# Attention scores: whole 32-row K tiles against zero-padded query copies, in place of a shifted copy of K

## The chip, the cores and the metric

The kernel runs on one NeuronCore of a Trainium2 chip. The metric is the device time of one execution in microseconds (us). The core has five engines that run in parallel and meet at semaphores: TensorE (PE in the profile) multiplies matrices into the eight banks of PSUM, VectorE (DVE), ScalarE (ACT) and GpSimd (POOL) compute elementwise, and SyncE (SP) here only issues DMAs. In the profile, PEld is the loading of a matmul's stationary operand. The granted clock is the share of its full speed that TensorE was given.

## The reference

Two blocks over the same x (2048 rows, 512 columns, bf16), mixed by a gate per row:

```python
x = A_x
g = _sigmoid((x * gate_w).sum(-1, keepdims=True))
a = _A_ref(x, A_wqkv, A_wo)
b = _B_ref(x, B_wqkv, B_wo)
return g * a + (1 - g) * b
```

A is softmax attention with 32 heads of 16 dimensions:

```python
qkv = (lambda x, *d: x.transpose(*d))((x @ wqkv).reshape(B, S, 3, H, Dh), 2, 0, 3, 1, 4)
q, k, v = qkv[0], qkv[1], qkv[2]
scores = jnp.einsum("bhqd,bhkd->bhqk", q, k) * (Dh ** -0.5)
p = _softmax(scores, axis=-1)
o = jnp.einsum("bhqk,bhkd->bhqd", p, v)
```

B is linear attention with the feature map phi(t) = t + 1 where t > 0, exp(t) elsewhere, plus 1e-6. Both end in an output projection.

## The kernel before

**Layout.** K is kept transposed in KT: four groups (t8) of 128 partitions, eight heads of 16 rows each, for all 2048 keys. A query tile QT holds the same for one group and 512 queries; there are 16 query tiles, counted by q4, in three buffers. A score matmul takes 16 rows of K and of Q, at partitions 0, 32, 64 or 96, so that up to four heads run side by side in the rows of the array, each writing 128 keys x 512 queries into a PSUM bank of its own.

**Two rounds to a query tile.** The four heads that start at partitions 0, 32, 64 and 96 are one round (`par` 0). The other four start at 16, 48, 80 and 112, where a tile of the array cannot begin. For them one DMA per group copies KT, shifted by 16 partitions, into KS (`t_kproj`), and one per query tile copies QT into QS (`t_qproj`); round `par` 1 reads KS and QS (`kq_aps`). A KS copy is made when all four key quarters of a group are projected, so an odd round needs all of them (`kq_keys`). There are 32 rounds of 16 key blocks and four heads: 2048 score matmuls.

**What follows a score.** ACT takes three banks, then two, in turn, and writes exp into a PT buffer (line 806). For some key blocks DVE does the exponential instead: line 982 evicts a bank as scaled integers into Lb, and lines 1004 to 1014 make Eb and Xb from it, so that three products with V (and with a scaled copy VX) together give what PT would. The PV matmuls take 128 keys as rows and 17 columns (16 of V and a one for the sum), four heads side by side in the columns of the array, and accumulate in one bank (`acc`). At the end of a round DVE transposes, divides and gates (`round_end`).

**The order** is not written by hand. While the program is built, a planner holds a clock for each engine with fixed costs, and picks what TensorE does next: score groups for ACT first, then scores for DVE, PV, products for DVE's blocks, and projections and all of block B as tasks with a due time and an earliest time, both counted in rounds. A query tile is due at 2 q4 - 0.9. Where the next pick lies in the future and fewer than WARMC columns were streamed in the last 3.413 us of the planner's clock, it emits a dummy: four PV-shaped matmuls on a tile of zeros (`emit_dummy`, tile sb_warm), which add zero. The plan is fixed in the program; on the chip each engine runs its own list in order and waits at semaphores.

Of the kernel before, what the change touches and what calls it, by code (L numbers as in the profile page):

```python
# [145 lines left out]
def bass_gated_mix__mha_block__linear_attn_block__prompt_kernel(  # L146
# [26 lines left out]
    with ExitStack() as es:  # L173
# [33 lines left out]
        identb = SB("identb", [128, 128], BF16)  # L207
        pidx_i = SB("pidx_i", [128, 1], I32)
        pidx = SB("pidx", [128, 1], FP32)
        mtmp = SB("mtmp", [128, 8], FP32)  # L210
# [40 lines left out]
        r_KT = [[R(f"KT{a}_{t}") for t in range(4)] for a in range(4)]  # L251
        r_KS = [R(f"KS{a}") for a in range(4)]
        r_QT = [R(f"QT{a}") for a in range(3)]
        r_QS = [R(f"QS{a}") for a in range(3)]
        r_V = [[R(f"V{k}_{g}") for g in range(2)] for k in range(NTB)]
# [124 lines left out]
        op(PO, lambda: nc.gpsimd.memset(warm, 0.0), writes=[r_warm])  # L380
        op(PO, lambda: nc.gpsimd.memset(dummy[:], 0.0), writes=[r_dummy])  # L381
        op(PO, lambda: nc.gpsimd.memset(identb[:], 0.0), writes=[r_ident])
# [4 lines left out]
        op(PO, lambda: nc.gpsimd.iota(pidx_i[:], [[0, 1]], base=0, channel_multiplier=1), writes=[r_mask])  # L387
        op(PO, lambda: nc.gpsimd.tensor_copy(pidx[:], pidx_i[:]), reads=[r_mask], writes=[r_mask])
        for j in range(8):
# [39 lines left out]
        def t_kproj(t8, t):  # L429
            if t8 == 0:  # L430
                lhs, wr = (lambda cc: wA0[:, 0, cc, :]), r_wA0
            else:
                lhs, wr = (lambda cc: wA[:, 1, cc, 128 * t8:128 * (t8 + 1)]), r_wA[1]
            b = yield "bank"
            yield from proj_steps(b, lhs, lambda cc: xT[:, cc, 512 * t:512 * (t + 1)], [r_xT[c][t] for c in range(NCC)] + [wr])
            yield ("dve", [r_bk[b]], [])
            op(DV, lambda: nc.vector.tensor_copy(KT[:, t8, 512 * t:512 * (t + 1)], BK[b]), reads=[r_bk[b]],  # L437
               writes=[r_KT[t8][t]], cost=0.69)
            yield "free"
            if t == 3:  # L440
                dma(KS[0:112, t8, :], KT[16:128, t8, :], f"ks{t8}", reads=r_KT[t8], writes=[r_KS[t8]], lat=4)

        def t_qproj(qc, t8):
            s = (4 * qc + t8) % 3
            if t8 == 0 and qc == 0:
                lhs, wr = (lambda cc: wA0[:, 1, cc, :]), r_wA0
# [3 lines left out]
            yield from proj_steps(b, lhs, lambda cc: xT[:, cc, 512 * qc:512 * (qc + 1)], [r_xT[c][qc] for c in range(NCC)] + [wr])  # L450
            yield ("dve", [r_bk[b]], [r_QT[s]])
            op(DV, lambda: nc.vector.tensor_copy(QT[:, s, :], BK[b]), reads=[r_bk[b]], writes=[r_QT[s]], cost=0.69)
# [185 lines left out]
        DLAT, DGRACE = 10.5, 2.0  # L638
        WARMC = 3400.0

# [410 lines left out]
        for t in range(NQC):  # L1051
            add(("xtr", t), t_xtr(t), 0.25 * t - 0.3)
            add(("K", 0, t), t_kproj(0, t), 0.25 * t - 0.2, pre=[("xtr", t)] + ([("K", 0, k) for k in range(3)] if t == 3 else []))
            if t == 0:
# [8 lines left out]
        for t8 in range(1, 4):  # L1063
            for t in range(4):
                add(("K", t8, t), t_kproj(t8, t), 2 * t8 - 0.9 + 0.1 * t, 2 * t8 - 1.8 + 0.2 * t,
                    pre=XT + ([("K", t8, k) for k in range(3)] if t == 3 else []))
        for q4 in range(1, 16):
# [150 lines left out]
```

## Time and profile before

| | |
|---|---|
| Times of the runs | 1076.32 and 1089.12 us, median 1082.72 |
| Profiled execution | 1079.47 us, span in its trace 1077.7 us |
| Busy share of the span | PE 92%, ACT 77%, DVE 63%, weight loads 19%, POOL 2% |
| Mean granted clock of TensorE | 0.587 of full |
| Score matmuls | 1024 on QT and KT, 1024 on QS and KS, mean 553 and 568 ns |
| Exponentials on ACT | 687 instructions, 815.9 us |
| Blocks of exponentials on DVE | 83, with 332 score tiles |
| Dummy matmuls | 516 |
| DMA | 16.39 MB, 16 engines mostly idle |

Busy times overlap, since the engines run side by side. Matmuls are pipelined: four tiles side by side each show some 0.4 to 0.6 us, and the busy time of a group counts a stretch once. A share over the whole span is a mean over stretches that may be limited by different things. Some records of matmuls can be missing from a trace; the weight loads show how many there were.

### The profile page before, as it was taken

The numbers are of one execution on the slowest core, as the hardware profiler recorded it, in microseconds if no ns is written. First come the engines' busy times: TensorE is split into PE (matmuls) and PEld (weight loads), VectorE is DVE, ScalarE is ACT, GpSimd is POOL, SyncE is SP. The second block draws the span as 40 slices with busy tenths as digits, with TensorE's granted clock in tenths as the row PEclk, the third lists the DMA queues.
The fourth block names the chain that finished last, engine by engine and source line by source line (L and its number), as shares of the span: only waits on it lengthen the run. The fifth ranks groups of instructions, "written<-read, shape, count | busy, mean of one in ns | idle before, by whom it ended". The sixth has DMA issues, their size and how long they took to land. (4 is left out here: it accounts for less than half of the span.)

```text
span 1077.7 us, 14346 instructions
## 1 busy us (share of the span) xinstructions
PE 993.1 (92%) x6101; PEld 209.9 (19%) x6164; DVE 678.0 (63%) x1003; ACT 833.3 (77%) x722; POOL 17.5 (2%) x43
## 2 busy tenths in 40 slices
PE   6999899899998998998989999999999999899998
PEld 2312111111111111212112112222221211111112
DVE  2335766676767667745556667766665664766775
ACT  4874787887877878968777888958877787687995
POOL 2101100000000000000000000000000000000000
PEclk9755855655555556658655555865585655655556
DMA  7000000000000000001001000000000000000000
GB/s 190 18 5 17 5 18 1 22 1 5 1 5 1 1 5 2 25 1 44 1 1 44 1 6 9 21 16 1 17 18 15 3 16 17 10 5 18 4 1 20
DMA packets 29487, 16.39 MB, mean 15 GB/s; under 512 B 16944, under 2 KB 28976, under 8 KB 29424
## 3 DMA queue, kind: packets, MB, share of 16 engines
q1 hardware_dynamic: 25232, 13.64, 4.6%
q10 hardware_dynamic: 4192, 1.84, 0.7%
q8 instruction: 48, 0.79, 0.3%
q14 instruction: 15, 0.12, 0.0%
HBM read 6.55 MB, written 2.10 MB: 8 GB/s over the span
## 5 line engine op out<-in xcount | busy, mean ns | idle before, releaser
L806 ACT ACTIVATE sb_PT<-ps 128x1536 bf16<-128x1536 f32 (+1 forms) x687 | 815.9, 1248 | 212.1 <-PE ps L357 207.0
L982 DVE TENSOR_SCALAR sb_Lb<-ps 128x512 uint16<-128x512 f32 x332 | 225.0, 689 | 270.8 <-PE ps L357 269.5
L357 PE MATMUL ps<-sb_QT,sb_KT 16*128 16x512 bf16 x1024 | 240.9, 553 | 17.7 <-ACT sb_PT L806 11.8
L357 PE MATMUL ps<-sb_QS,sb_KS 16*128 16x512 bf16 x1024 | 240.2, 568 | 14.4 <-ACT sb_PT L806 11.8
L357 PE MATMUL ps<-sb_PT,sb_V 128*17 128x512 bf16 x1716 | 236.8, 554 | 8.9 <-DVE sb_U L879 8.3
L1014 DVE TENSOR_TENSOR sb_Xb<-sb_Xb,sb_Lb 128x2048 bf16<-128x2048 bf16 x83 | 101.6, 1224 | 2.4
L1011 DVE TENSOR_TENSOR sb_Xb<-sb_Xb 128x2048 bf16<-128x2048 bf16 x83 | 101.1, 1219 | 0.0
L357 PEld LDWEIGHTS ps<-sb_QT,sb_KT 16*128 16x128 bf16 x1024 | 42.6, 98 | 213.0 <-ACT sb_PT L806 100.2
L357 PEld LDWEIGHTS ps<-sb_PT,sb_V 128*17 128x17 bf16 x1716 | 41.3, 91 | 198.8 <-issue 174.2
L357 PEld LDWEIGHTS ps<-sb_QS,sb_KS 16*128 16x128 bf16 x1024 | 41.4, 98 | 197.2 <-ACT sb_PT L806 96.9
L357 PE MATMUL ps<-sb_warm 128*17 128x512 bf16 (+1 forms) x524 | 74.2, 602 | 1.3 <-POOL sb_dummy L381 1.3
L1007 DVE TENSOR_SCALAR sb_Eb<-sb_Lb 128x2048 uint16<-128x2048 uint16 x83 | 57.0, 686 | 0.0
L1004 DVE TENSOR_SCALAR sb_Xb<-sb_Lb 128x2048 uint16<-128x2048 uint16 x83 | 56.7, 683 | 0.0
L357 PE MATMUL ps<-sb_Lb,sb_V 128*17 128x512 bf16 x332 | 48.1, 576 | 6.0 <-DVE sb_Lb L982 5.4
L357 PE MATMUL ps<-sb_Xb,sb_VX 128*17 128x512 bf16 x332 | 48.1, 570 | 4.1 <-DVE sb_Xb L1014 4.1
L357 PE MATMUL ps<-sb_Eb,sb_V 128*17 128x512 bf16 x332 | 49.0, 580 | 1.0 <-DVE sb_Eb L1007 0.9
L357 PE MATMUL ps<-sb_xT,sb_wA 128*128 128x512 bf16 x92 | 41.2, 556 | 5.4 <-issue 3.4
L357 PE MATMUL ps<-sb_wBx,sb_xT 128*128 128x512 bf16 x50 | 25.9, 608 | 4.7 <-issue 2.3
L879 DVE STREAM_TRANSPOSE sb_U<-ps 128x512 f32<-128x512 f32 x32 | 22.8, 711 | 10.4 <-PE ps L357 10.1
L357 PE MATMUL ps<-sb_wA,sb_xT 128*128 128x128 bf16 (+1 forms) x128 | 27.7, 362 | 1.7 <-DVE sb_Lb L982 1.7
L357 PE MATMUL ps<-sb_phiK,sb_xnat 128*128 128x512 bf16 x56 | 26.6, 581 | 2.6 <-issue 2.0
L437 DVE CAST sb_KT<-ps 128x512 bf16<-128x512 f32 x16 | 11.0, 689 | 27.4 <-PE ps L357 27.4
(74 smaller groups left out, 377.2 us busy)
## 6 DMA issues: line engine op xcount, KB each, us to landing
out_dram<-sb_wA SPq DMA_DIRECT2D x16, 128.0 KB, 1.7
sb_QS<-sb_QT SPq DMA_DIRECT2D x16, 112.0 KB, 2.1
sb_KS<-sb_KT SPq DMA_DIRECT2D x4, 448.0 KB, 3.4
sb_xnat<-in_A_x_dram ACTq DMA_DIRECT2D x2, 512.0 KB, 5.2
sb_wA<-in_A_wqkv_dram SPq DMA_DIRECT2D x2, 512.0 KB, 5.3
sb_wBx<-in_B_wqkv_dram SPq DMA_DIRECT2D x2, 512.0 KB, 5.3
sb_xnat<-in_A_x_dram SPq DMA_DIRECT2D x2, 512.0 KB, 3.9
sb_phiK<-sb_wA SPq DMA_TRANSPOSE x64, 2.2
```

Of the source, the lines that this page charges most:

```text
L357: return lambda: nc.tensor.matmul(o, lhsT=l, rhs=r, start=start, stop=stop, skip_group_check=sg)
L437: op(DV, lambda: nc.vector.tensor_copy(KT[:, t8, 512 * t:512 * (t + 1)], BK[b]), reads=[r_bk[b]], writes=[r_KT[t8][t]], cost=0.69)
L806: op(AC, lambda: nc.scalar.activation(PT[:, slot, 0:512 * n], ps[:, 512 * set_[0]:512 * (set_[0] + n)], ACT.Exp, scale=SCALE), reads=wr, w ...
L879: op(DV, lambda: nc.vector.transpose(U[:], acc), reads=[r_acc], writes=[r_U], cost=0.69)
L982: ev = op(DV, lambda: nc.vector.tensor_scalar(Lb[:, sl, 512 * j:512 * (j + 1)], BK[b], S1A, S1B, op0=ALU.mult, op1=ALU.add), reads=[r_bk[b ...
L1004: ev = op(DV, lambda: nc.vector.tensor_scalar(X, L, 0x7F, 0x3F80, op0=ALU.bitwise_and, op1=ALU.bitwise_or), reads=[rl], writes=[rx], cost= ...
L1007: ev = op(DV, lambda: nc.vector.tensor_scalar(E_, L, 0xFF80, None, op0=ALU.bitwise_and), reads=[rl], writes=[re_], cost=CH[1])
L1011: ev = op(DV, lambda: nc.vector.tensor_tensor(xb, xb, xb, ALU.mult), reads=[rx], writes=[rx], cost=CH[2])
L1014: ev = op(DV, lambda: nc.vector.tensor_tensor(xb, xb, lb, ALU.mult), reads=[rx, rl], writes=[rx], cost=CH[3])
```

## The change

**Scores.** KS and QS go. A score matmul now takes all 32 rows of a K tile, which are two heads, for both rounds (`kq_aps`). The query side is QP, with two copies per query tile: in copy p only the 16 rows of the heads of round p hold the query, the other 16 of each 32 are zero, so the other head's rows add nothing.

**How QP is filled.** QP is set to zero once at the start. For 15 of the 16 query tiles, DVE copies the projection into a staging buffer QT (now two), and eight DMAs from SP's queue lay strips of 16 rows into the two copies. The very first tile is written without DMA, by two DVE multiplications with 0/1 masks of the rows, which four small DVE instructions make from an index that POOL now produces earlier.

**Dependencies and planner.** An odd round needs only the quarter of K that it reads, and the last quarter of a group no longer waits for the other three. WARMC goes from 3400 to 3550. The planner then makes another plan.

```diff
@@ SBUF tiles, start @@
-        KS = SB("KS", [128, 4, S], BF16)
-        QT = SB("QT", [128, 3, 512], BF16)
-        QS = SB("QS", [128, 3, 512], BF16)
+        QT = SB("QT", [128, 2, 512], BF16)
+        QP = SB("QP", [128, 3, 2, 512], BF16)
+        maskp = SB("maskp", [128, 2], FP32)
...
+        op(DV, lambda: nc.vector.memset(QP[:], 0.0), writes=[x for v in r_QP for x in v], cost=0.9)
+        op(DV, lambda: nc.vector.tensor_scalar(pidx_j[:], pidx_i[:], 16, None, op0=ALU.bitwise_and),
+           reads=[r_mask], writes=[r_maskp])
+        op(DV, lambda: nc.vector.tensor_copy(maskp[:, 0:1], pidx_j[:]), reads=[r_maskp], writes=[r_maskp])
...
@@ t_kproj @@
-            if t == 3:
-                dma(KS[0:112, t8, :], KT[16:128, t8, :], f"ks{t8}", reads=r_KT[t8], writes=[r_KS[t8]], lat=4)
@@ t_qproj @@
-            yield ("dve", [r_bk[b]], [r_QT[s]])
-            op(DV, lambda: nc.vector.tensor_copy(QT[:, s, :], BK[b]), reads=[r_bk[b]], writes=[r_QT[s]], cost=0.69)
+            if n == 0:
+                yield ("dve", [r_bk[b], r_maskp], [])
+                for p in range(2):
+                    op(DV, lambda p=p: nc.vector.tensor_scalar(QP[:, s, p, :], BK[b], maskp[:, p:p + 1], None, op0=ALU.mult),
+                       reads=[r_bk[b], r_maskp], writes=[r_QP[s][p]], cost=0.69)
+                yield "free"
+                return
+            yield ("dve", [r_bk[b]], [r_QT[st]])
+            op(DV, lambda: nc.vector.tensor_copy(QT[:, st, :], BK[b]), reads=[r_bk[b]], writes=[r_QT[st]], cost=0.69)
             yield "free"
-            dma(QS[0:112, s, :], QT[16:128, s, :], f"qs{s}", reads=[r_QT[s]], writes=[r_QS[s]], lat=2.5)
+            for p in range(2):
+                for j in range(4):
+                    lo = 32 * j + 16 * p
+                    dma(QP[lo:lo + 16, s, p, :], QT[lo:lo + 16, st, :], f"qp{s}_{p}", reads=[r_QT[st]],
+                        writes=[r_QP[s][p]] if j == 0 else [], lat=2.5)
+                r_QP[s][p].w = _Raw(dma_sems[f"qp{s}_{p}"][0], dma_sems[f"qp{s}_{p}"][1], SP.clock + 2.5)
+                r_QP[s][p].r = {}
@@ planner @@
-        WARMC = 3400.0
+        WARMC = 3550.0
...
-            return [("K", t8, kb // 4) if par == 0 else ("K", t8, 3), ("Q", qc, t8)]
+            return [("K", t8, kb // 4), ("Q", qc, t8)]
...
-            if par == 0:
-                return (KT[32 * j:32 * j + 16, t8, 128 * kb:128 * (kb + 1)], QT[32 * j:32 * j + 16, s, :], [r_KT[t8][kb // 4], r_QT[s]])
-            return (KS[32 * j:32 * j + 16, t8, 128 * kb:128 * (kb + 1)], QS[32 * j:32 * j + 16, s, :], [r_KS[t8], r_QS[s]])
+            return (KT[32 * j:32 * j + 32, t8, 128 * kb:128 * (kb + 1)], QP[32 * j:32 * j + 32, s, par, :],
+                    [r_KT[t8][kb // 4], r_QP[s][par]])
```

**How the lists of the engines move.** First TensorE, in the fourth round, at one of block B's first projections (sb_wBx); sb_PT, sb_Lb and sb_Eb are the PV products, sb_warm the dummies. Before:

```order
L357 MATMUL ps<-sb_wBx,sb_xT 128x512 x4
L357 MATMUL ps<-sb_QS,sb_KS 128x512 x4
L357 MATMUL ps<-sb_PT,sb_V 17x512 x4
L357 MATMUL ps<-sb_QS,sb_KS 128x512 x6
L357 MATMUL ps<-sb_PT,sb_V 17x512 x4
L357 MATMUL ps<-sb_Lb,sb_V 17x512 x4
L357 MATMUL ps<-sb_QS,sb_KS 128x512 x2
L357 MATMUL ps<-sb_PT,sb_V 17x512 x4
L357 MATMUL ps<-sb_Eb,sb_V 17x512 x4
L357 MATMUL ps<-sb_warm 17x512 x8
```

After, TensorE at the same place:

```order
L358 MATMUL ps<-sb_wBx,sb_xT 128x512 x4
L358 MATMUL ps<-sb_QP,sb_KT 128x512 x4
L358 MATMUL ps<-sb_PT,sb_V 17x512 x4
L358 MATMUL ps<-sb_QP,sb_KT 128x512 x3
L358 MATMUL ps<-sb_warm 17x512 x4
L358 MATMUL ps<-sb_QP,sb_KT 128x512 x3
L358 MATMUL ps<-sb_PT,sb_V 17x512 x4
L358 MATMUL ps<-sb_Lb,sb_V 17x512 x4
L358 MATMUL ps<-sb_QP,sb_KT 128x512 x2
L358 MATMUL ps<-sb_PT,sb_V 17x512 x4
L358 MATMUL ps<-sb_Eb,sb_V 17x512 x4
L358 MATMUL ps<-sb_warm 17x512 x4
```

The work is the same; one dummy has moved ahead into the six scores. Over the program the dummies go from 516 to 588 matmuls, and the scores for DVE's blocks from 332 to 328.

Second SP, whose whole list is DMAs, after the loads of the inputs. Before:

```order
L302 DMA sb_QS<-sb_QT 112x512
L302 DMA sb_KS<-sb_KT 112x2048
L302 DMA sb_QS<-sb_QT 112x512
L302 DMA sb_KS<-sb_KT 112x2048
L302 DMA sb_QS<-sb_QT 112x512
L302 DMA sb_KS<-sb_KT 112x2048
L302 DMA sb_QS<-sb_QT 112x512
L302 DMA sb_KS<-sb_KT 112x2048
L302 DMA sb_QS<-sb_QT 112x512 x4
L302 DMA sb_wBx<-in_B_wqkv_dram 128x4x512
```

After, SP from the same place, up to the loads of the output weights:

```order
L303 DMA sb_QP<-sb_QT 16x512 x56
L303 DMA sb_wBx<-in_B_wqkv_dram 128x4x512
L303 DMA sb_xnat<-in_A_x_dram 128x8x256 x2
L303 DMA sb_QP<-sb_QT 16x512 x16
L303 DMA sb_phiK<-in_A_wo_dram 128x4x512
L303 DMA sb_phiK<-in_B_wo_dram 128x4x512
```

Eight query copies and four K copies ahead of the reload of sb_wBx become 56 strips for seven query tiles; the first tile needs none.

Third DVE, from its first instruction on; sb_QP is the query copies, sb_maskp and sb_pidx_j the masks. Before:

```order
L397 MEMSET ps 128x512
L398 MEMSET sb_V 128x512
L425 COPY sb_xT<-ps 128x512 x2
L437 CAST sb_KT<-ps 128x512
L452 CAST sb_QT<-ps 128x512
L465 CAST sb_V<-ps 128x4x8x16
```

After, DVE at the same place:

```order
L398 MEMSET ps 128x512
L399 MEMSET sb_QP 128x1536
L400 TENSOR_SCALAR sb_pidx_j<-sb_pidx_i 128x1
L402 CAST sb_maskp<-sb_pidx_j 128x1
L403 TENSOR_SCALAR sb_maskp<-sb_maskp 128x1
L405 TENSOR_SCALAR sb_maskp<-sb_maskp 128x1
L407 MEMSET sb_V 128x512
L434 COPY sb_xT<-ps 128x512 x2
L446 CAST sb_KT<-ps 128x512
L462 TENSOR_SCALAR sb_QP<-ps,sb_maskp 128x512 x2
L486 CAST sb_V<-ps 128x4x8x16
```

Five instructions come in ahead of the first copy of x, and the first query takes two instructions where it took one.

More of the change, by code (lines that the diff above doesn't have):

```diff
@@ L208, in bass_gated_mix__mha_block__linear_attn_block__prompt_kernel @@
         pidx_i = SB("pidx_i", [128, 1], I32)
+        pidx_j = SB("pidx_j", [128, 1], I32)
         pidx = SB("pidx", [128, 1], FP32)
@@ L251, in bass_gated_mix__mha_block__linear_attn_block__prompt_kernel @@
         r_KT = [[R(f"KT{a}_{t}") for t in range(4)] for a in range(4)]
-        r_KS = [R(f"KS{a}") for a in range(4)]
-        r_QT = [R(f"QT{a}") for a in range(3)]
-        r_QS = [R(f"QS{a}") for a in range(3)]
+        r_QT = [R(f"QT{a}") for a in range(2)]
+        r_QP = [[R(f"QP{a}_{p}") for p in range(2)] for a in range(3)]
+        r_maskp = R("maskp")
         r_V = [[R(f"V{k}_{g}") for g in range(2)] for k in range(NTB)]
@@ L381, in bass_gated_mix__mha_block__linear_attn_block__prompt_kernel @@
         op(PO, lambda: nc.gpsimd.memset(dummy[:], 0.0), writes=[r_dummy])
+        op(PO, lambda: nc.gpsimd.iota(pidx_i[:], [[0, 1]], base=0, channel_multiplier=1), writes=[r_mask])
         op(PO, lambda: nc.gpsimd.memset(identb[:], 0.0), writes=[r_ident])
@@ L386, in bass_gated_mix__mha_block__linear_attn_block__prompt_kernel @@
         op(PO, lambda: nc.gpsimd.memset(ones[:], 1.0), writes=[r_const])
-        op(PO, lambda: nc.gpsimd.iota(pidx_i[:], [[0, 1]], base=0, channel_multiplier=1), writes=[r_mask])
         op(PO, lambda: nc.gpsimd.tensor_copy(pidx[:], pidx_i[:]), reads=[r_mask], writes=[r_mask])
@@ L439, in t_kproj @@
             yield "free"
-            if t == 3:
-                dma(KS[0:112, t8, :], KT[16:128, t8, :], f"ks{t8}", reads=r_KT[t8], writes=[r_KS[t8]], lat=4)
         def t_qproj(qc, t8):
-            s = (4 * qc + t8) % 3
-            if t8 == 0 and qc == 0:
+            n = 4 * qc + t8
+            s, st = n % 3, n % 2
+            if n == 0:
                 lhs, wr = (lambda cc: wA0[:, 1, cc, :]), r_wA0
@@ L1052, in bass_gated_mix__mha_block__linear_attn_block__prompt_kernel @@
             add(("xtr", t), t_xtr(t), 0.25 * t - 0.3)
-            add(("K", 0, t), t_kproj(0, t), 0.25 * t - 0.2, pre=[("xtr", t)] + ([("K", 0, k) for k in range(3)] if t == 3 else []))
+            add(("K", 0, t), t_kproj(0, t), 0.25 * t - 0.2, pre=[("xtr", t)])
             if t == 0:
@@ L1065, in bass_gated_mix__mha_block__linear_attn_block__prompt_kernel @@
                 add(("K", t8, t), t_kproj(t8, t), 2 * t8 - 0.9 + 0.1 * t, 2 * t8 - 1.8 + 0.2 * t,
-                    pre=XT + ([("K", t8, k) for k in range(3)] if t == 3 else []))
+                    pre=XT)
         for q4 in range(1, 16):
```

5 lines of the change are left out of this document (added).

## The prediction

> **What bounds the kernel now.** First the page: the share of each engine, the slices and the chain of waits.
>
> ```profile
> span 1077.7 us, 14346 instructions
> PE 993.1 (92%) x6101; PEld 209.9 (19%) x6164; DVE 678.0 (63%) x1003; ACT 833.3 (77%) x722; POOL 17.5 (2%) x43
> PEclk9755855655555556658655555865585655655556
> PE 36%; ACT 6%; DVE 3%; issue 1%
> ```
>
> TensorE is busy for 92% and leads the chain, yet at what clock: most slices stand at five tenths. So I read the busy time of each engine in stretches cut where the granted clock changes; the columns are the stretch, its length, PE, weight loads, DVE, ACT, POOL, the granted clock, DMA share and GB/s. The first sum is over ten stretches at full clock, of which the first, the last and one between are shown; the second is over six at half clock, with the last of them.
>
> ```profile
> 14.00:38.00 24.00, 20.58 (x213) 9.33 (x214) 7.69 (x15) 22.14 (x20) 1.59 (x3) 1.00 0.34 107
> 683.20:707.00 23.80, 21.94 (x169) 5.77 (x168) 16.53 (x23) 23.49 (x23) 0.00 (x0) 1.00 0.09 24
> 925.50:935.70 10.20, 8.67 (x77) 2.50 (x77) 8.59 (x15) 7.75 (x8) 0.00 (x0) 1.00 0.05 14
> sum 136.10, PE 116.81 PEld 35.97 DVE 93.11 ACT 126.77 POOL 1.59; mean PE 11.68 PEld 3.60 DVE 9.31 ACT 12.68 POOL 0.16
> ...
> 935.80:1068.00 132.20, 125.78 (x805) 23.09 (x805) 93.18 (x133) 111.44 (x95) 0.00 (x0) 0.50 0.03 6
> sum 587.80, PE 553.01 PEld 102.70 DVE 396.56 ACT 472.81 POOL 0.00; mean PE 92.17 PEld 17.12 DVE 66.09 ACT 78.80 POOL 0.00
> ```
>
> At half clock PE is full and ACT, which does the exponentials, works 472.81 / 587.80 = 80% of the time; at full clock PE has room and ACT works 93%, in the second row 99%. The kernel has two regimes: PE-bound at half clock, for most of the run, and ACT-bound at full clock. What decides is the clock, so I looked for what raises it. The clock changes only at edges 3.41 us apart; three such windows at half clock, each with the row behind it that shows what it earned:
>
> ```profile
> 335.00:338.41 3.41, 3.39 (x30) 0.72 (x30) 2.14 (x5) 2.20 (x2) 0.00 (x0) 0.50 0.00 0
> 338.41:341.82 3.41, 2.04 (x23) 0.54 (x23) 3.03 (x4) 2.72 (x4) 0.00 (x0) 1.00 0.02 5
> 591.00:594.41 3.41, 3.41 (x30) 0.65 (x23) 1.64 (x4) 2.52 (x3) 0.00 (x0) 0.50 0.00 0
> 594.41:597.83 3.42, 3.01 (x25) 0.61 (x21) 3.42 (x5) 3.23 (x3) 0.00 (x0) 0.50 0.01 2
> 922.09:925.51 3.42, 3.04 (x22) 0.70 (x23) 2.35 (x2) 0.00 (x0) 0.00 (x0) 0.50 0.02 5
> 925.51:928.92 3.41, 3.41 (x34) 1.06 (x33) 2.86 (x6) 0.97 (x2) 0.00 (x0) 1.00 0.00 0
> ```
>
> The first and second both hold 30 matmuls and a full PE; one is followed by the full clock, the other is not. The third has fewer matmuls and an idle gap, and the clock rises. What they consist of, by groups, window by window (a group counts a matmul that reaches over an edge):
>
> ```profile
> L357 PE MATMUL ps<-sb_PT,sb_V 128*17 128x512 bf16 x16 | 2.1, 614 | 0.8 <-DVE sb_U L879 0.8
> L357 PE MATMUL ps<-sb_QS,sb_KS 16*128 16x512 bf16 x10 | 1.4, 550 | 0.0
> L357 PE MATMUL ps<-sb_Lb,sb_V 128*17 128x512 bf16 x4 | 0.6, 632 | 0.0
> ...
> L357 PE MATMUL ps<-sb_QS,sb_KS 16*128 16x512 bf16 x14 | 2.1, 614 | 0.0
> L357 PE MATMUL ps<-sb_PT,sb_V 128*17 128x512 bf16 x12 | 1.5, 620 | 0.0
> L357 PE MATMUL ps<-sb_Lb,sb_V 128*17 128x512 bf16 x4 | 0.6, 632 | 0.0
> ...
> L357 PE MATMUL ps<-sb_warm 128*17 128x512 bf16 x12 | 1.5, 632 | 0.0
> L357 PE MATMUL ps<-sb_phiK 128*128 128x512 bf16 x1 | 0.6, 634 | 0.3 <-issue 0.3
> L357 PE MATMUL ps<-sb_Eb,sb_V 128*17 128x512 bf16 x4 | 0.6, 597 | 0.8 <-DVE sb_Eb L1007 0.8
> L357 PE MATMUL ps<-sb_Xb,sb_VX 128*17 128x512 bf16 x4 | 0.4, 388 | 0.0
> ```
>
> Call 512 columns over the whole array a wave: four PV tiles (17 columns, 128 rows each) are one, a whole-array matmul is one, and four score tiles (16 rows each) count w. The first window has 5 + 2.5 w and rises; the second 4 + 3.5 w and does not; the third has 5 waves of tiles, three of them the dummies, plus one or two whole matmuls, and rises. With w = 1 the second would have 7.5 and stay cold where the third rises on little over 6. So w is below 1, and w = 0.5 fits all three (6.25, 5.75, 6.1 or more) with a threshold of about 6 waves per window. Half is what 16 rows of a 32-row tile are. The dummies are all zeros and still count, so it is active rows, not values.
>
> **The change part by part.** *Score tiles.* Each reads 32 rows instead of 16, the extra ones zero in the query. Their own duration should not move:
>
> ```profile
> L357 PE MATMUL ps<-sb_QT,sb_KT 16*128 16x512 bf16 x1024 | 240.9, 553 | 17.7 <-ACT sb_PT L806 11.8
> L357 PE MATMUL ps<-sb_QS,sb_KS 16*128 16x512 bf16 x1024 | 240.2, 568 | 14.4 <-ACT sb_PT L806 11.8
> L357 PE MATMUL ps<-sb_PT,sb_V 128*17 128x512 bf16 x1716 | 236.8, 554 | 8.9 <-DVE sb_U L879 8.3
> L357 PE MATMUL ps<-sb_warm 128*17 128x512 bf16 x516 | 70.6, 602 | 0.0
> L357 PE MATMUL ps<-sb_Eb,sb_V 128*17 128x512 bf16 x332 | 49.0, 580 | 1.0 <-DVE sb_Eb L1007 0.9
> ```
>
> 16-row tiles take 553 to 568 ns and 128-row tiles 554: rows cost no time. What moves is w, to 1 if active rows are what counts. Tiles: 2048 + 1716 + 516 + 3 x 332 = 5276, or 1319 waves; the 825 other recorded matmuls I take as 500 waves (many are short). Before, with w = 0.5: 1819 - 256 = 1563 waves in 1077.7 / 3.41 = 316 windows, 4.95 each, well under 6. After: 18 dummy waves more (588 dummy matmuls in the program against 516), some 1835, which at the old pace are 5.8 per window, at the edge, so that cold windows now and then pass (the second window above would have 7.5), and at a pace of 925 us 6.8, above it. The half clock can no longer hold for long and the full clock can, though attention-only stretches stay near 6 and will fall back at times. I take the cold state to be left in one window of three and the warm one lost in one of nine: a warm share of 0.75. The bounds are 0.5 and 1.
>
> *The sum.* ACT's work is 833.3 us, and one block of DVE exponentials goes back to it (328 tiles in the program instead of 332): four tiles at 1462 / 3 = 487 ns, 1.9 us, so 835.2, of which 1.6 lie in the first row below.
>
> ```profile
> L806 ACT ACTIVATE sb_PT<-ps 128x1536 bf16<-128x1536 f32 x343 | 501.6, 1462 | 144.8 <-PE ps L357 142.8
> 0.00:16.00 16.00, 8.64 (x34) 3.31 (x35) 3.20 (x6) 1.62 (x3) 5.54 (x29) 1.00 0.99 230
> 1066.00:1077.70 11.70, 8.38 (x39) 3.35 (x36) 4.96 (x9) 0.00 (x0) 0.00 (x0) 0.88 0.13 45
> 112.80 1.02 ACT L806 ACTIVATE sb_PT<-ps 128x1024 bf16<-128x1024 f32 x1 [14.41 <-PE ps L357]
> ```
>
> Outside it lie 16.0 us of start, 11.7 of end and one gap of 14.4 while PE does a row of V projections, which I put at 10 at the faster clock. What is left of before, 1077.7 - 42.1 = 1035.6, holds 136.1 at a share of 0.93 and so 899.5 at (833.3 - 1.6 - 126.8) / 899.5 = 0.784. After, with a warm share of 0.945 (between the mean of 0.93 and the 0.99 of the longest), 0.75 x 0.945 + 0.25 x 0.784 = 0.905, and 833.6 / 0.905 = 921. With 37.7 of start, end and gap: 959. The profiled execution took 1079.47 us, 1.8 above its span, and lies 0.3% under the median of 1082.72: forecast 961. Bounds, with the same 39.5 around them: warm throughout at 0.985, 846 and so 886; half the time at 0.93, 833.6 / 0.857 = 973 and so 1012.
>
> *Query strips.* Eight DMAs from SP in place of one, for 15 of the 16 query tiles; the four K copies go.
>
> ```profile
> 501.85 0.69 DVE L452 CAST sb_QT<-ps 128x512 bf16<-128x512 f32 x1 [1.54 <-PE ps L357]
> 502.57 0.52 SPq L302 DMA_DIRECT2D sb_QS<-sb_QT  x1
> sb_QS<-sb_QT SPq DMA_DIRECT2D x16, 112.0 KB, 2.1
> 538.14 0.10 PEld L357 LDWEIGHTS ps<-sb_QT,sb_KT 16*128 16x128 bf16 x1
> 5.84 0.42 DVE L425 COPY sb_xT<-ps 128x512 bf16<-128x512 bf16 x1 [2.21 <-PE ps L422]
> ```
>
> Issue costs 8 x 0.52 = 4.2 us and the last lands 2.1 later: 6.3 us after the cast at 501.85. The tile cast there is first loaded at 538.14, some 35 us on; at the faster clock that shrinks to 30 and still covers it. Behind the strips on SP stand the next strips, three reloads of weights and inputs, output transposes and stores, none of which a row shows PE waiting for. Cost 0; without cover, 15 x 6.3 = 95 us. Odd rounds no longer ask for all of K; no row shows PE waiting for that copy, so it gains 0. *Start.* The memset of QP and four mask operations fit before the copy at 5.84, ahead of which DVE idled 2.21 us; the first query costs a second 0.69 us on DVE, behind the half that round 0 needs. Between 0 and 2 us, taken as 0.
>
> **The rivals.** *The clock does not move.* Row tiling itself could be what counts half, however many rows; no 32-row tile is in the trace to exclude it. Then PE stays the bound and the 18 dummy waves cost up to 70.6 / 129 = 0.55 us each, 10 us: 1089. Chance 0.11. The Trainium skill speaks for this case (TensorE: Matmul & The Clock Gate, Part 1): it has the clock released by how busy PE has been in windows of about 3.4 us, and asks only for PE without long gaps. By that rule rows would change nothing and the sum would be the 1089 of this case, by the row reading 961. The trace bears out the window and contradicts the rest: PE was busy 125.78 of 132.20 us at 0.50.
>
> *Rows count, but the full clock does not hold* in the attention stretches: warm share 0.25 to 0.5, 1012 to 1060. Chance 0.06.
>
> *Slower: tiles stop overlapping.* In the score waves of TensorE, four 16-row tiles run side by side; 32-row tiles fill their row groups to the border, and a weight load for one could hold up its neighbour. With 512 waves, 42 ns each are 21.6 us, the 2% from which it decides; 0.2 us each are 103 us, 1180. Against it: PV tiles fill all 128 rows of their columns, and 30 tiles of either kind, some 0.6 us each, fit into one window of 3.41 us. Chance 0.04.
>
> **How the numbers follow.** The forecast, rows counted and the clock mostly full, has 0.79, its own range 886 to 1012. 2% is about what a measurement of this kernel tells from no change, so faster means under 1061: 0.79 + 0.06 = 0.85; same 0.11; slower 0.04. The range from 895 to 1060 leaves out 0.11 + 0.04 and some 0.04 of the forecast's fast end.
>
> **What would show it.** The mean granted clock near 0.85 instead of a little under 0.6; the score groups' mean well under 500 ns instead of 560; ACT at 85 to 88% of the span; half-clock stretches of a few windows, mostly between rounds without projections; no idle time put down to the QP DMAs. A clock near 0.6 with w still 0.5 refutes the reading of rows; a full clock with ACT under 90% in it refutes the sum.

## The result, and the profile after

The changed kernel takes 928.59 us (median of two runs, 926.35 and 930.83) against 1082.72: a ratio of 0.8576, with a 95% interval of 0.8341 to 0.8812. It lies inside the forecast's own range and 32 us under the 961. The profiled execution is the run of 930.83, 1.8 us above its span; its mean granted clock is 0.838 where it was 0.587. Ratios, here and below, compare the faster executions of each kernel alone, while the times are medians over all of them, so a ratio can differ a little from the quotient of the two times.

First the page of the changed kernel: busy time of each engine, the clock in 40 slices, the chain of waits, and four groups.

```profile
span 929.0 us, 14661 instructions
PE 801.4 (86%) x6228; PEld 203.3 (22%) x6228; DVE 670.8 (72%) x1001; ACT 809.3 (87%) x723; POOL 16.6 (2%) x43
PEclk9989889979687867789757999997788789977856
ACT 56%; PE 34%; DVE 7%; issue 2%; DMA 1%; ACTq 0%; DVEq 0%
L826 ACT ACTIVATE sb_PT<-ps 128x1536 bf16<-128x1536 f32 (+1 forms) x688 | 796.9, 1306 | 93.9 <-PE ps L358 91.9
L358 PE MATMUL ps<-sb_QP,sb_KT 32*128 32x512 bf16 x2048 | 357.6, 444 | 84.5 <-ACT sb_PT L826 73.6
L358 PE MATMUL ps<-sb_PT,sb_V 128*17 128x512 bf16 x1720 | 192.6, 449 | 10.1 <-DVE sb_U L899 8.5
L358 PE MATMUL ps<-sb_warm 128*17 128x512 bf16 (+1 forms) x596 | 63.9, 466 | 1.3 <-POOL sb_dummy L382 1.3
```

PE does the same work and more dummies in 801.4 us instead of 993.1, and every kind of matmul shares in it: PV tiles, which the change does not touch, go from 554 to 449 ns. That is a clock, not a cheaper instruction. The chain of waits now runs mostly through ACT (56%, before 6%), and most of PE's idle time is waiting for ACT to hand back a bank (73.6 of 84.5 us ahead of the scores, before 23.6 of 32.1).

Next the same kernel cut where the granted clock changes: the sum over all stretches at full clock, the sum over all at half, both from 16.0 us on; then the rows of start and end. The columns are those of the stretches shown before. The trace's record of the clock begins at 16.0 us (at 14.2 us in the kernel before), and what lies ahead of it is printed as 1.00: that figure in the row of the start is no reading (weight loads come every 0.43 us there, the pace of half clock, as the last section shows), and it lifts the mean clocks by up to 0.01.

```profile
sum 612.62, PE 503.44 PEld 143.82 DVE 469.86 ACT 569.51 POOL 8.53; mean PE 14.81 PEld 4.23 DVE 13.82 ACT 16.75 POOL 0.25
...
sum 300.42, PE 289.84 PEld 56.34 DVE 196.72 ACT 238.31 POOL 2.55; mean PE 8.78 PEld 1.71 DVE 5.96 ACT 7.22 POOL 0.08
...
0.00:16.00 16.00, 8.09 (x25) 3.07 (x26) 4.19 (x10) 1.49 (x2) 5.51 (x29) 1.00 1.00 194
917.00:929.00 12.00, 9.09 (x36) 3.52 (x36) 4.95 (x9) 0.00 (x0) 0.00 (x0) 0.85 0.13 45
```

And the gap of ACT while the V projections run, in its timeline (start, length, in brackets the idle time ahead):

```profile
94.09 2.54 ACT L826 ACTIVATE sb_PT<-ps 128x1024 bf16<-128x1024 f32 x2 [11.69 <-PE ps L358]
```

And of the kernel before, all stretches at full clock and all at half, where the prediction had only ten and six of them (from 14.2 us on):

```profile
sum 172.64, PE 140.94 PEld 43.55 DVE 120.83 ACT 146.67 POOL 7.16; mean PE 7.83 PEld 2.42 DVE 6.71 ACT 8.15 POOL 0.40
...
sum 890.88, PE 844.78 PEld 163.46 DVE 554.69 ACT 685.12 POOL 4.77; mean PE 49.69 PEld 9.62 DVE 32.63 ACT 40.30 POOL 0.28
```

The full clock went from 172.64 of 1063.5 us to 612.62 of 913.0 us. Inside each state PE is much as it was: at half clock 844.78 / 890.88 = 95% busy before and 289.84 / 300.42 = 96% after, at full clock 82% in both. What the change moved is how long each state lasts.

### The profile page after: what moved, and what is told of

It is laid out like the page before. It is cut to its first block, busy times and chain, and to the rows that moved or that the text cites. A ratio compares the mean times of both kernels' runs of the same rounds, so it can differ in the third digit from the quotient of the medians.

```text
span 929.0 us, 14661 instructions
## 1 busy us (share of the span) xinstructions
PE 801.4 (86%) x6228; PEld 203.3 (22%) x6228; DVE 670.8 (72%) x1001; ACT 809.3 (87%) x723; POOL 16.6 (2%) x43
## 4 chain that ended last, share of the span: by engine, by line
ACT 56%; PE 34%; DVE 7%; issue 2%; DMA 1%; ACTq 0%; DVEq 0%
ACT sb_PT L826 54%; PE ps L358 34%; DVE sb_Lb L1002 2%; ACT sb_ebuf L528 1%; DMA sb_OT<-in_A_wqkv_dram 1%; DVE sb_Xb L1034 1%; DVE sb_Xb L1031 1%; DVE sb_U L899 1%; DVE sb_Eb L1027 0%; DVE sb_wA L646 0%; DVE sb_xnat L532 0%; DVE sb_Xb L1024 0%; DVE sb_ebuf L530 0%; DVE sb_V L495 0%; DVE sb_phiK L532 0%
## 5 line engine op out<-in xcount | busy, mean ns | idle before, releaser
L826 ACT ACTIVATE sb_PT<-ps 128x1536 bf16<-128x1536 f32 (+1 forms) x688 | 796.9, 1306 | 93.9 <-PE ps L358 91.9
L358 PE MATMUL ps<-sb_QP,sb_KT 32*128 32x512 bf16 x2048 | 357.6, 444 | 84.5 <-ACT sb_PT L826 73.6
L358 PE MATMUL ps<-sb_PT,sb_V 128*17 128x512 bf16 x1720 | 192.6, 449 | 10.1 <-DVE sb_U L899 8.5
L358 PEld LDWEIGHTS ps<-sb_QP,sb_KT 32*128 32x128 bf16 x2048 | 79.1, 93 | 381.8 <-ACT sb_PT L826 263.1
L358 PE MATMUL ps<-sb_warm 128*17 128x512 bf16 (+1 forms) x596 | 63.9, 466 | 1.3 <-POOL sb_dummy L382 1.3
L358 PE MATMUL ps<-sb_Xb,sb_VX 128*17 128x512 bf16 x328 | 38.0, 453 | 11.1 <-DVE sb_Xb L1034 10.9
L358 PE MATMUL ps<-sb_Eb,sb_V 128*17 128x512 bf16 x328 | 38.0, 453 | 2.4 <-DVE sb_Eb L1027 2.2
L528 ACT ACTIVATE sb_ebuf<-ps 128x512 f32<-128x512 f32 x32 | 21.4, 669 | 3.0 <-PE ps L358 3.0
L646 DVE CAST sb_wA<-ps 128x512 bf16<-128x512 f32 x16 | 10.9, 688 | 16.1 <-PE ps L358 16.1
L358 PE MATMUL ps<-sb_phiK 128*128 128x512 bf16 x64 | 21.5, 439 | 0.0
```

What stands on the lines that cost most here:

```text
L358: return lambda: nc.tensor.matmul(o, lhsT=l, rhs=r, start=start, stop=stop, skip_group_check=sg)
L528: op(AC, lambda: nc.scalar.activation(ebuf[:, s, :], BK[b], ACT.Exp), reads=[r_bk[b]], writes=[r_e[s]], cost=0.68)
L646: op(DV, lambda: nc.vector.tensor_copy(outt[:, sl, :], BK[b]), reads=[r_bk[b]], writes=[r_outt[sl], r_wA[2]], cost=0.69)
L826: op(AC, lambda: nc.scalar.activation(PT[:, slot, 0:512 * n], ps[:, 512 * set_[0]:512 * (set_[0] + n)], ACT.Exp, scale=SCALE), reads=wr, w ...
```

## The experiments

The theory: a matmul counts for the clock by the rows of the array that it fills, so that a 16-row score counts half of what it streams and a 32-row one all of it; a window of 3.41 us with about 6 counted waves earns the full clock for the next. Rivals: the new plan and its other DMAs and dummies bring the gain; or PE's busy time decides, whatever it streams; or what counts is the values that pass, not the rows.

### The change without its rows

The changed kernel with its lists, strips and dummies as they are, but score matmuls that read 16 rows. In odd rounds the upper heads' scores are thereby replaced by those of the lower ones.

```diff
-            return (KT[32 * j:32 * j + 32, t8, 128 * kb:128 * (kb + 1)], QP[32 * j:32 * j + 32, s, par, :],
-                    [r_KT[t8][kb // 4], r_QP[s][par]])
+            return (KT[32 * j:32 * j + 16, t8, 128 * kb:128 * (kb + 1)], QP[32 * j:32 * j + 16, s, 0, :],
+                    [r_KT[t8][kb // 4], r_QP[s][0], r_QP[s][par]])
```

> The changed kernel with its instruction lists unchanged on every engine, except that every score matmul reads 16 rows in place of 32, of the even heads in both rounds (odd heads' scores are replaced by the even heads', so the attention of odd heads is not computed). Theory A, active rows set the clock: back to the half clock, mean granted clock 0.57 to 0.63, a score tile weighs 0.5, and the time returns to 1070 to 1100 us. Rival B, the gain comes from the new plan, its 18 more dummy waves, the freed order of K and the strips: all of them are still there, so 920 to 940 us and a clock of 0.83.

Measured: 1079.52 us against 1069.25 for the kernel before on the same chip, a ratio of 1.0017 (0.9823 to 1.0211). Its page:

```profile
span 1056.1 us, 14591 instructions
PE 969.4 (92%) x6167; PEld 208.6 (20%) x6228; DVE 675.2 (64%) x1001; ACT 831.8 (79%) x723; POOL 16.6 (2%) x43
PEclk9798558555585555556655555766568565855556
PE 71%; ACT 18%; DVE 7%; issue 2%; DMA 1%; ACTq 0%; DVEq 0%
L358 PE MATMUL ps<-sb_QP,sb_KT 16*128 16x512 bf16 x2048 | 428.9, 547 | 32.9 <-ACT sb_PT L826 25.7
```

The lists are instruction for instruction those of the changed kernel, and the whole gain is gone: the clock is back at 0.619, the chain back on PE. Plan, strips, masks and the 72 dummies more are together worth nothing that this comparison can see. Two windows at half clock show it in small, each with the row behind it, and then the groups of matmuls in the first. The changed kernel, windows:

```profile
94.53:97.94 3.41, 3.41 (x30) 0.67 (x26) 2.09 (x5) 2.88 (x3) 0.00 (x0) 0.50 0.00 0
97.94:101.36 3.42, 3.42 (x28) 1.00 (x25) 1.78 (x3) 3.39 (x4) 0.00 (x0) 1.00 0.00 0
```

Its groups:

```profile
L358 PE MATMUL ps<-sb_PT,sb_V 128*17 128x512 bf16 x16 | 2.2, 605 | 0.0
L358 PE MATMUL ps<-sb_QP,sb_KT 32*128 32x512 bf16 x10 | 1.8, 592 | 0.0
L358 PE MATMUL ps<-sb_Lb,sb_V 128*17 128x512 bf16 x4 | 0.6, 632 | 0.0
```

The 16-row kernel, windows:

```profile
870.27:873.68 3.41, 3.41 (x30) 0.69 (x26) 2.64 (x5) 2.98 (x3) 0.00 (x0) 0.50 0.00 0
873.68:877.09 3.41, 3.37 (x24) 0.64 (x23) 3.38 (x4) 3.13 (x4) 0.00 (x0) 0.50 0.02 5
```

Its groups:

```profile
L358 PE MATMUL ps<-sb_PT,sb_V 128*17 128x512 bf16 x16 | 2.0, 552 | 0.0
L358 PE MATMUL ps<-sb_QP,sb_KT 16*128 16x512 bf16 x10 | 1.8, 603 | 0.0
L358 PE MATMUL ps<-sb_Lb,sb_V 128*17 128x512 bf16 x4 | 0.6, 632 | 0.0
```

Both windows hold 16 + 10 + 4 matmuls and a PE busy for all of 3.41 us; the one with 32 rows earns the full clock, the one with 16 does not. One such pair is an illustration, no proof: a group counts matmuls that reach over an edge, and the prediction's first window had these same counts with 16 rows and did rise. Cut at the edges, it held 20 PV tiles and 7.3 scores, this one 16 and 9.3: 5.9 and 5.2 counted waves. Hence the count over all windows, further down.

### The rows without the rest of the change

The kernel before, its plan and its shifted copies as they are, but score matmuls of 32 live rows. Each score is then the sum over two heads. Two memsets on POOL at the start fill the rows that the copies leave unwritten with zeros, so that in odd rounds one tile in four has 16 live rows.

```diff
+        op(PO, lambda: nc.gpsimd.memset(QS[96:128], 0.0), reads=[r_const], writes=r_QS)
+        op(PO, lambda: nc.gpsimd.memset(KS[96:128], 0.0), reads=[r_QS[0]], writes=r_KS)
...
-                return (KT[32 * j:32 * j + 16, t8, 128 * kb:128 * (kb + 1)], QT[32 * j:32 * j + 16, s, :], [r_KT[t8][kb // 4], r_QT[s]])
-            return (KS[32 * j:32 * j + 16, t8, 128 * kb:128 * (kb + 1)], QS[32 * j:32 * j + 16, s, :], [r_KS[t8], r_QS[s]])
+                return (KT[32 * j:32 * j + 32, t8, 128 * kb:128 * (kb + 1)], QT[32 * j:32 * j + 32, s, :], [r_KT[t8][kb // 4], r_QT[s]])
+            return (KS[32 * j:32 * j + 32, t8, 128 * kb:128 * (kb + 1)], QS[32 * j:32 * j + 32, s, :], [r_KS[t8], r_QS[s]])
```

> The kernel before with its lists unchanged on PE, DVE, ACT and SP, except that score matmuls read 32 rows of KT, QT, KS and QS without zeros (each score becomes the sum over two heads, so the attention's values change; two memsets on GpSimd at the start fill the last 16 rows of the shifted copies). Theory A: the clock rises as in the changed kernel, mean 0.78 to 0.84, and the time falls to 930 to 970 us, a little above the changed kernel because 18 dummy waves are missing. If in addition only zero-padded rows did something, or the plan did (rival B): 1075 to 1095 us at a clock of 0.59.

Measured: 911.40 us, a ratio of 0.8645 (0.8532 to 0.8759); clock 0.872, from its page:

```profile
span 905.2 us, 14350 instructions
PE 758.6 (84%) x6101; PEld 203.1 (22%) x6164; DVE 673.6 (74%) x1003; ACT 804.0 (89%) x722; POOL 25.0 (3%) x45
PEclk8879879999985899889978888799899899957968
```

The rows alone give the whole gain, with the old copies and 516 dummies. The time lies below the 930 to 970 us that were expected: that 72 dummies are missing cost nothing that shows here. With the run above it is settled from both sides: the rows are needed and they suffice.

### Three quarters of the rows, and rows without zeros

Two runs ask what it is about the rows. The first takes 24 of them (in odd rounds half of each head's dimensions are left out). The second makes the strips carry all 32 rows of the projection, so that no row of the query is zero and each score is the sum over two heads; for that the masks of the first tile become one as well (not shown below). Beside it the changed kernel itself ran again on the second one's chip.

```diff
-            return (KT[32 * j:32 * j + 32, t8, 128 * kb:128 * (kb + 1)], QP[32 * j:32 * j + 32, s, par, :],
+            return (KT[32 * j:32 * j + 24, t8, 128 * kb:128 * (kb + 1)], QP[32 * j:32 * j + 24, s, par, :],
```

> The changed kernel with its lists unchanged, score matmuls over 24 of the 32 rows (in even rounds the result is the same, in odd rounds half of each head's dimensions are left out). Theory A with every active row counting (a score tile weighs 0.75): between the two, 980 to 1030 us, clock 0.68 to 0.76. If a tile counts as a whole from some number of rows on: 925 to 940 us when 24 is enough, 1070 to 1100 us when only all 32 do.

```diff
-                    dma(QP[lo:lo + 16, s, p, :], QT[lo:lo + 16, st, :], f"qp{s}_{p}", reads=[r_QT[st]],
+                    dma(QP[32 * j:32 * j + 32, s, p, :], QT[32 * j:32 * j + 32, st, :], f"qp{s}_{p}", reads=[r_QT[st]],
```

> The changed kernel with its lists unchanged, but the strips carry all 32 rows and the first tile's masks are one, so that no row of a query copy is zero (each score is the sum over two heads). If only active rows count, whatever they hold: the time of the changed kernel within 1%, 905 to 930 us, clock 0.82 to 0.86. If zeros count for less, which would explain why the kernel before with 32 live rows ran at 0.872: 895 to 912 us, clock 0.86 to 0.89.

> The changed kernel itself, as the measure for the runs beside it. 905 to 930 us, clock 0.82 to 0.86, a warm share of about two thirds.

Measured: 24 rows 1026.82 us, ratio 0.9661 (0.9412 to 0.9911), clock 0.666, between 16 rows (0.619) and 32 (0.838), though in the traced execution below the 0.68 that was expected at least. Live rows 927.20 us, ratio 0.8722 (0.8606 to 0.8839), clock 0.836, against 926.05 us, 0.8651 (0.8520 to 0.8783), for the changed kernel beside it. The intervals overlap. So whether half of the rows hold zeros makes no difference that these runs can tell: rows count by being addressed. The weight load and the stream of a score always address the same rows here, so which of the two counts is not separated.

### The count over all windows

For each half or full window of a trace I added up what was streamed in it, each matmul's 512 columns laid out from its weight load on and cut at the edges, in waves as the prediction defines them, with a weight w for the score tiles. Then I looked for the one threshold that best sorts the windows into those followed by the full clock and those followed by the half. The table gives how many windows are sorted wrongly.

| Kernel | score rows | windows | wrong, w = 0.5 | wrong, w = 0.75 | wrong, w = 1 | threshold at the best w, waves |
|---|---|---|---|---|---|---|
| before | 16 | 314 | 3 | 4 | 11 | 5.99 |
| after's lists, 16 rows | 16 | 307 | 0 | 4 | 11 | 5.97 |
| after's lists, 24 rows | 24 | 299 | 7 | 5 | 7 | 6.05 |
| before, 1252 dummies (below) | 16 | 315 | 1 | 6 | 13 | 5.96 |
| after | 32 | 270 | 15 | 11 | 3 | 5.92 |
| before's plan, 32 rows | 32 | 263 | 15 | 6 | 5 | 5.85 |
| after, no zero rows | 32 | 270 | 17 | 11 | 5 | 5.94 |

In each kernel the fewest are wrong at w = rows / 32, in some by one or two windows only, and with that weight the threshold is the same everywhere, 5.85 to 6.05. The few windows that remain wrong lie near the threshold, and the ends of matmuls are modelled. The three weights are a quarter apart. In finer steps the same traces have the fewest wrong at 0.45 to 0.7 with 16 rows, near 0.8 with 24 and at 0.9 to 1.1 with 32, so the weight follows the rows, within 0.1 or 0.2. The columns were taken to count in full, four tiles of 17 columns as one wave, and the traces bear that out: with a weight of 17/32 for these tiles and the best threshold for it, 17 to 37 windows of each kernel would be wrong.

### The dummies

If 6 counted waves are what a window needs, dummies could supply them. Each of these runs changes the planner's bound WARMC and nothing else in the code; the number of dummy matmuls in the program follows from it. The planner then makes another plan, so other work can move a little too. First the bound of the changed kernel in the kernel before, 600 dummies for 516:

```diff
-        WARMC = 3400.0
+        WARMC = 3550.0
```

> The kernel before with only WARMC at 3550 (600 dummy matmuls in place of 516). Theory A: 21 dummy waves at half clock cost up to 11 us and earn a few windows of full clock, 1065 to 1095 us, clock 0.58 to 0.63. Rival B, more dummies are what keeps the clock: 920 to 960 us.

Measured: 1077.06 us, 1.0157 (1.0059 to 1.0255), clock 0.614: no gain from more dummies, if anything a loss. Then the changed kernel with WARMC at 0, 3400, 4000, 4500 and 5500 in place of 3550:

> The changed kernel planned with WARMC 0: no dummy matmuls at all, 147 waves fewer. Theory A: attention-only stretches then hold about 0.5 waves per window less and stay cold much more, warm share 0.35 to 0.5, 960 to 1010 us. If the dummies earn nothing: their 147 x 0.4 us saved where PE is the bound, 890 to 920 us.

> The changed kernel planned with the old WARMC of 3400: 480 dummy matmuls, 27 waves fewer. Theory A: on the line between no dummies (952 us) and 588 of them (926 us), 925 to 940 us, clock 0.79 to 0.83. If the plan for 3400 is better by itself, which the run of the kernel before with 32 rows at 911 us would suggest: 905 to 920 us.

> The changed kernel planned with WARMC 4000: 896 dummy matmuls in place of 588, 77 waves more. Theory A: at full clock PE has room for them and the clock falls back less often, warm share 0.75 to 0.95, 880 to 912 us. If more dummies only take time: 77 x 0.3 to 0.5 us, 940 to 960 us.

> The changed kernel planned with WARMC 4500: 1252 dummy matmuls, 166 waves more than at 3550. Theory A: the clock stays full in nearly every window, warm share above 0.93, ACT bounds the kernel, 868 to 890 us. If dummies begin to stand in the way of PE: 895 to 915 us.

> The changed kernel planned with WARMC 5500: 1864 dummy matmuls, 319 waves more than at 3550. Theory A: nothing is left for the clock to gain; the added waves take 319 x 0.2 us or more of PE at full clock, 64 us, some of it in the way of scores: 875 to 905 us, not better than 4500.

| WARMC | dummy matmuls | us, median | ratio to before | clock | half-clock windows followed by full | full-clock windows followed by half |
|---|---|---|---|---|---|---|
| 0 | 0 | 952.34 | 0.9008 (0.8876 to 0.9140) | 0.715 | 0.22 | 0.31 |
| 3400 | 480 | 920.01 | 0.8559 (0.8496 to 0.8622) | 0.857 | 0.40 | 0.17 |
| 3550 (the change) | 588 | 926.05 | 0.8651 (0.8520 to 0.8783) | 0.823 | 0.37 | 0.19 |
| 4000 | 896 | 902.84 | not given (runs of 884.5 to 905.6) | 0.932 | 0.64 | 0.10 |
| 4500 | 1252 | 879.82 | 0.8186 (0.8138 to 0.8234) | 0.957 | 0.53 | 0.05 |
| 5500 | 1864 | 891.88 | 0.8298 (0.8251 to 0.8345) | 0.954 | 0.45 | 0.05 |

(The clock is that of the traced execution, one of three or four; the others had 0.741 and 0.748 without dummies, 0.828 to 0.862 at 3550 and 0.888 to 0.897 at 4000. The two shares of 3550 are from the profile shown first, the others each from the run's own. From 4000 on the share of half-clock windows rests on 20 to 35 of them.) Without dummies the time is below the 960 to 1010 us expected, with 480 of them just below the 925 to 940; the other three lie in their ranges. The version with 4500 beats both kernels: 879.82 us, by the two ratios 5% under the change. Its page:

```profile
span 876.8 us, 15932 instructions
PE 749.2 (85%) x6831; PEld 214.2 (24%) x6892; DVE 669.8 (76%) x1001; ACT 798.8 (91%) x723; POOL 18.4 (2%) x43
ACT 77%; PE 14%; DVE 5%; issue 2%; DMA 1%; ACTq 0%; DVEq 0%
```

Its sums over the stretches at full clock and at half:

```profile
sum 797.19, PE 679.23 PEld 195.32 DVE 625.85 ACT 750.54 POOL 12.29; mean PE 56.60 PEld 16.28 DVE 52.15 ACT 62.54 POOL 1.02
...
sum 75.10, PE 66.77 PEld 17.87 DVE 42.13 ACT 48.24 POOL 3.03; mean PE 6.07 PEld 1.62 DVE 3.83 ACT 4.39 POOL 0.28
```

More than twice the dummies, and PE is busy for 52 us less than in the changed kernel, since nearly everything runs at full clock. ACT is the bound at 91%. At 5500 the dummies begin to cost: PE is busy 786.7 us at the same clock, and the time is 12 us longer.

If counted waves were all, the same dummies should lift the kernel before as well. So the last run gives it 4500, with 16 rows:

> The kernel before, 16 rows, planned with WARMC 4500: 1252 dummy matmuls, 184 waves more than it had. Theory A counts waves: its 512 score waves at half weight and 313 dummy waves make some 1790 counted waves, between the changed kernel without dummies (some 1740, 952 us) and with 588 (some 1890, 926 us): 930 to 955 us, clock 0.70 to 0.80. If 32 rows did something of their own that dummies cannot replace: 1060 to 1100 us.

Measured: 1065.64 us against 1070.59, a ratio of 0.9805 (0.9740 to 0.9870), clock 0.632 in the traced execution of 1083.38 us; the quickest of the twelve took 1037.82 us at 0.690. The dummies gain 2% here, and the expectation was missed by over 100 us. The line of its page:

```profile
PE 1027.0 (95%) x6892; PEld 222.2 (21%) x6892; DVE 673.2 (62%) x995; ACT 834.4 (77%) x723; POOL 18.4 (2%) x43
```

A stretch from the middle of the run, and the sums at full clock and at half:

```profile
300.00:440.00 140.00, 138.11 (x849) 24.68 (x845) 92.30 (x133) 110.62 (x97) 0.00 (x0) 0.51 0.01 3
...
sum 281.97, PE 241.58 PEld 69.92 DVE 207.76 ACT 239.16 POOL 10.27; mean PE 15.10 PEld 4.37 DVE 12.99 ACT 14.95 POOL 0.64
...
sum 795.30, PE 782.38 PEld 151.22 DVE 464.48 ACT 595.22 POOL 5.24; mean PE 52.16 PEld 10.08 DVE 30.97 ACT 39.68 POOL 0.35
```

For 140 us the profile has PE busy 99%, and the clock stays at half. The reason stands in the means of the windows:

| Kernel | half-clock window: streamed waves | of these counted | followed by full | full-clock window: followed by half |
|---|---|---|---|---|
| before, 516 dummies | 5.55 | 4.76 | 0.06 | 0.37 |
| before, 1252 dummies | 5.79 | 5.02 | 0.06 | 0.17 |
| after, 16 rows | 5.59 | 4.78 | 0.08 | 0.30 |
| after, 24 rows | 5.61 | 5.22 | 0.14 | 0.31 |
| after | 5.59 | 5.59 | 0.37 | 0.19 |
| before's plan, 32 rows | 5.61 | 5.61 | 0.43 | 0.15 |

At half clock PE is the bound, and what it streams in a window moves little with the plan: 5.55 waves with 516 dummies in the kernel before, 5.79 with 1252. Most of a dummy does not come on top there, it pushes other work into the next window. With 16-row scores these 5.79 waves count 5.02, and the window that would reach 6 stays rare (0.06). With 32 rows all 5.6 count, the mean lies just under the threshold, and every second or third window passes. Here dummies do help: without any, the share of half-clock windows that pass is 0.22 instead of 0.37. At full clock PE has room, dummies come on top, and they keep the clock: the share of windows that lose it falls with their number in both kernels, with 32 rows from 0.31 without any to 0.05. So the half clock is a trap. Rows lead out of it, 736 more dummies did not lead the 16-row kernel out, and dummies keep the kernel from falling back in.

## Why the prediction was right, point by point

**The clock as the cause, and w.** Right. w = 0.5 and a threshold of about 6 waves, read from three windows, hold over 314 (5.99, three wrong), and w goes to 1 with 32 rows, as forecast. Three windows were thin ground: the groups count matmuls that reach over an edge, and cut there the three hold 5.9, 5.5 and 6.1 counted waves. The one that stays cold still has the least, and with that the reading stands. The rival of the clock that does not move is refuted by both runs on the rows. The Trainium skill (TensorE: Matmul & The Clock Gate, Part 1: The HAM clock gate), from which that rival took its rule, has the clock follow how busy PE was in windows of 3413 ns: the edges agree (3.41 us), as do the two states of half and full, but busy time as the profile has it does not decide, with 138.11 of 140 us at 0.51 in the last run.

**The argument by pace failed.** The prediction set 6.8 waves a window "at a pace of 925 us" against 5.8 at the old one, and counted the 18 dummy waves more toward them. A mean over the run is not what a window at half clock can stream: it was 5.59, hardly more than the 5.55 before. What changed is that all of it counts. (The other matmuls, put at 500 waves, hold 549 by the weight loads; that moves neither side of the argument.) By the failed step, 1252 dummies should have freed the 16-row kernel, and they did not.

**A warm share of 0.75 from one in three and one in nine.** Leaving was right (0.37 of the half-clock windows). Losing was not: 0.19, not 0.11. Between start and end and without the gap, the full clock held for 595.4 of 889.3 us, a share of 0.67.

**The sum.** Forecast, 833.6 / 0.905 + 37.7 = 959 of span. Measured, start 16.0, end 12.0 and gap 11.7 make 39.7, and the 889.3 us between hold 569.51 + 238.31 = 807.8 us of ACT, a share of 0.908. The share came out right by luck, from two errors that cancel: less time at full clock, but ACT denser in it (569.51 / 595.4 = 0.956 where 0.945 was taken) and at half clock (238.31 / 293.9 = 0.811 where it was 0.784). What was mis-sized is ACT's work: taken as fixed at 835.2, it was 809.3. That is (833.6 - 807.8) / 0.905 = 28.5 us; the share gives 3.3 back, the ends and the gap cost 2.0 more: 959 - 28.5 - 3.3 + 2.0 = 929.

The cause shows between two kernels with the same lists, the changed one and the one of 16 rows, in their groups of exponentials:

```profile
L826 ACT ACTIVATE sb_PT<-ps 128x1536 bf16<-128x1536 f32 (+1 forms) x688 | 816.0, 1252 | 195.2 <-PE ps L358 190.4
```

There, at a clock of 0.619, 688 exponentials take 816.0 us of busy time, in the changed kernel the same 688 take 796.9, though each record is longer (1306 against 1252 ns). 688 x 1.306 = 899 us in 796.9: the records overlap, an exponential starts before the one ahead of it has ended, and it does so more often where ACT does not wait (78% of them in the changed kernel, 50% in the other). The two rows that the prediction quoted show it already, had I divided: 23.49 us for 23 instructions at full clock, 1.02 each, against 111.44 for 95 at half, 1.17.

**Tiles of 32 rows cost no time.** Right. Scores at half clock took 592 ns in the window above, 550 to 614 in those before; 30 tiles still fit into a window. The rival of lost overlap is refuted.

**The strips, taken as nothing.** Right: 120 of them land in 1.8 us at the median (first row below, from the DMA issues), and no wait of PE for their DMA is in the trace. The start, taken as nothing within 0 to 2 us, cost some 1.5: the first exponential stands at 17.40 (second row, ACT's timeline), before at about 15.9. The gap, put at 10, took 11.69.

```profile
sb_QP<-sb_QT SPq DMA_DIRECT2D x120, 16.0 KB, 1.8
```

```profile
17.40 1.45 ACT L826 ACTIVATE sb_PT<-ps 128x1536 bf16<-128x1536 f32 x1 [5.12 <-PE ps L358]
```

**What was to show it.** A clock near 0.85 (0.838), scores well under 500 ns (444), ACT at 85 to 88% of the span (87%), no idle time on the DMAs of QP: all as named. The half-clock stretches are short, two windows at the median and eight at most; that they lie mostly between rounds without projections holds only in part, since 54% of their windows hold next to no whole-array matmuls, against 35% of those at full clock.

**Open.** Before's plan with 32 rows took 911 us where the change took 926, but their ratios on their chips, 0.8645 and 0.8651, have intervals that overlap, so a difference of the plans is not shown. Nor is it settled whether 480 dummies differ from 588: 920.01 us, 0.8559 (0.8496 to 0.8622), overlaps too.

## What to carry to other kernels

Where the granted clock switches between half and full, count what each window of 3.41 us streams, a row-tiled matmul by the rows that it addresses: here a tile of 32 rows, half of them zeros, made the kernel 14% shorter while no matmul took longer. Look at the two states apart: what led out of the half clock here (more rows in each column streamed) is not what chiefly helped to keep the full one (dummies in PE's idle time). 1252 dummies gained 2% with 16 rows; with 32 rows they took the time from 952 us without any to 880. Carry no engine's busy time from one regime into the other: divide it by its instructions in each.

## What the runs showed of the hardware that was not expected

- **A PE that the profile shows as full can stay at half clock.** 138.11 of 140 us busy at a clock of 0.51, since what it streamed mostly counted under 6 waves a window.
- **The weight follows the rows addressed**, near 0.5, 0.75 and 1 at 16, 24 and 32 rows of 32, and zeros in them count fully (927.20 us without, 926.05 us with them). Columns do not count in this way: four tiles of 17 columns count as much as a matmul over the whole array.
- **Half-clock windows stream 5.6 waves where 8 are possible.** At a recorded clock of 0.50, whole-array weight loads follow one another every 0.43 us, 8 in 3.41 us (the kernel before with 1252 dummies, ahead of its first scores; weight loads in time order):

```profile
11.87 0.15 PEld L357 LDWEIGHTS ps<-sb_xT,sb_OT 128*128 128x128 bf16 x1 [0.28 <-issue]
12.29 0.15 PEld L357 LDWEIGHTS ps<-sb_xT,sb_OT 128*128 128x128 bf16 x1 [0.28 <-issue]
```

  Score and PV tiles in turn do not reach that. The window of the changed kernel from 94.53 us on, whose groups stand further up, in time order:

```profile
94.52 0.61 PE L358 MATMUL ps<-sb_QP,sb_KT 32*128 32x512 bf16 x4
95.06 1.03 PE L358 MATMUL ps<-sb_PT,sb_V 128*17 128x512 bf16 x8
95.88 0.64 PE L358 MATMUL ps<-sb_Lb,sb_V 128*17 128x512 bf16 x4
96.45 0.61 PE L358 MATMUL ps<-sb_QP,sb_KT 32*128 32x512 bf16 x3
96.99 0.61 PE L358 MATMUL ps<-sb_PT,sb_V 128*17 128x512 bf16 x4
97.53 0.57 PE L358 MATMUL ps<-sb_QP,sb_KT 32*128 32x512 bf16 x3
```

  Eight PV tiles, two waves, are followed by the next PV tiles after 0.82 us, 0.41 each; where a score wave follows a PV wave or the other way round, 0.54 to 0.57 us pass from start to start. The Trainium skill (TensorEngine Tiling (Array Packing), Key Properties) states that a change of the tiling mode drains TensorE, which agrees with these pauses. And two of the three groups of scores hold three tiles where four fit. By an estimate from all half-clock windows of this trace (every matmul laid out at 0.43 us per 512 columns from its start), tiles stream for 2.73 of 3.41 us, and the scores fill 64% of the places in the time that they stream. So of the 2.4 missing waves some 1.6 are pauses, mostly where the kind of tile changes, and some 0.8 are empty places beside scores. No run took either away, so what an order with fewer changes and four scores at a time would earn is open.
- **ACT's busy time for the same 688 exponentials depends on how closely they follow**: 816.0 us at a clock of 0.619, 796.9 at 0.838, 791.1 with 1252 dummies at 0.957.
